# Order of the first stage in a retention and feed-forward kernel: token sums between the weight sums, clamps behind copies, a key transposed ahead of scores

## The chip, the cores and the metric

The kernel runs on one core of a Trainium2 chip. The metric is the device time of one execution in microseconds (us), the median of several runs. A profile of one further execution shows what every engine did: PE (matrix multiplies and transposes, with its weight loads as PEld), DVE (vector operations), ACT (scalar operations), POOL (GpSimd), and the DMA queues, of which SP's carries nearly all loads and stores.

## What is computed

The reference has two halves. The first is a retention layer over 8 batches, 8 heads, 576 positions and 64 values a head; its output becomes 4608 tokens of 512 values. The second is a feed-forward layer with a product of two projections.

```
scores = (q @ k.T) / sqrt(64)
ret    = (scores * Dmat) @ v        # Dmat[i, j] = gamma_h ** (i - j) for i >= j, else 0
x      = ret, heads side by side    # 4608 x 512
h      = ((x @ w1) * (x @ w2)) @ w3
out    = h @ w_out
```

The weights arrive as 64-bit floating point numbers, so the kernel has to convert them to 32 bits itself.

## The kernel before, in words

**Retention.** The 576 positions of a pair of batches are cut into five chunks, the first of 64 positions and four of 128. A *unit* g is one chunk of one pair (unit 0 to 4 are the first pair). `load` (L100) brings k, q and v of a unit by DMA from SP's queue, 512 KB each, into tiles of which there are two of each kind. The decay is split into factors: `scale` (L162) multiplies q and v by them, either as one POOL operation (L171) or as eight ACT operations (L169). `front` (L174) transposes k and q on PE (L184), eight transposes each, and copies the results to the tiles kT and qT with two ACT copies each (L187). `score` (L190) multiplies kT and qT (L199) and masks the scores on DVE (L202, four operations). `state` (L206) adds the unit's k and v to a running state on PE (L220) and copies it out on ACT (L224). `pv` (L227) makes the output of the unit from state, qT, masked scores and v (L248, L255), and ACT copies it to token tiles xT (L260).

**Weights.** `load_block` (L276) loads one block of raw weight words into one of five buffers, again by SP's queue. A generator, `conversion` (L358), turns a block into 32-bit numbers in five DVE steps: the exponent e (L319), the mantissa m in two steps (L323, L326), and the joining of both (L340, L349). Together with L326 it issues two clamps on ACT (L329, L330) that bound the exponent; L340 of the block needs them. From the fifth block on, the generator begins a block ahead: the three steps of block n + 1 come before the two last steps of block n, and behind the last one the load of a further block is issued (L353). `convert(n)` (L379) takes n steps; `convert_up_to(n)` goes on until n blocks are done.

**Up-projection.** The product with w1 and w2 is done by a Strassen-Winograd scheme of seven products for one third of a pair's tokens and one quarter `fp` of the columns. `strassen_weights(fp)` (L150) makes the weight sums S1, S2, S3, S4 on DVE (L152), with a `yield` after each two. `strassen_tokens` (L415) makes the four token sums T1, T2, T3, -T4 (L424), on POOL unless told otherwise. `up` (L433) issues the products in the order A11·B11, S2·T2, S3·T3, S1·T1, A22·(-T4), A12·B21, S4·B22, each of eight PE matmuls (L450); five of them are followed by a DVE sum (L455), and each such sum by `convert(conv)`, so that conversion is spread between the products, and by one entry of the list `aside`, which holds other work. Then DVE multiplies the two projections (L476), and a last `convert(conv)` follows (L477).

**Order.** Nothing is reordered by a scheduler: every engine runs its instructions in the order in which the program issues them and waits by semaphores for the others. The order of the first stage is written out by hand (L603 to L664). There PE's work alternates between units of the retention and calls of `up`; DVE has conversions, sums and masks; ACT has copies, clamps and scalings. PSUM tiles rotate through seven banks.

The part around the change, in its order: weight sums of the first quarter, `pv(1)`, the loads of unit 3, the token sums, the first `up`, the front of unit 2, the scores and state of unit 2, the front of unit 3, `pv(2)`, the loads of unit 4, state and scores of unit 3, the second `up`, `pv(3)`, and the front of unit 4.

Of the kernel before, what the change touches and what calls it, by code (L numbers as in the profile page):

```python
# [8 lines left out]
F32 = mybir.dt.float32  # L9
# [26 lines left out]
def kernel(  # L36
# [20 lines left out]
    P = 128  # L57
    NP = H // 2
# [3 lines left out]
    NC = (S + P - 1) // P  # L62
# [22 lines left out]
    pools = {}  # L85
# [46 lines left out]
    for c in (0, slice(1, NC)):  # L132
        n = short if c == 0 else P
# [8 lines left out]
    def A(fp, nm):  # L142

        h, m = divmod(fp, 2)
        if nm in ("S1", "S2", "S4"):
            return wS[h][:, ("S1", "S2", "S4").index(nm), m]
        r, f = {"A11": (0, 0), "A12": (1, 0), "A21": (0, 1), "S3": (0, 1), "A22": (1, 1)}[nm]
        return wA[h][:, :, 2 * r:2 * r + 2, m * QC + f * P:m * QC + f * P + P]

    def strassen_weights(fp):  # L150
        def tt(out, in0, in1, op):
            nc.vector.tensor_tensor(out=A(fp, out), in0=A(fp, in0), in1=A(fp, in1), op=op)  # L152

        tt("S1", "A21", "A22", ALU.add)
        tt("S2", "S1", "A11", ALU.subtract)
        yield
        tt("S3", "A11", "A21", ALU.subtract)
        tt("S4", "A12", "S2", ALU.subtract)
        live["S", fp] = True
        yield  # L160

    def scale(g, nm, scalar=False):  # L162
        c = g % NC
        sz = sizes[c]
        t, gam = live[nm, g], {"q": gq, "v": gk}[nm]
        t = t[:sz].rearrange("p (b h) d -> p b h d", b=2)
        if scalar:
            for h in range(H):
                nc.scalar.mul(t[:, :, h, :], t[:, :, h, :], gam[:sz, c, h:h + 1])  # L169
            return  # L170
        nc.gpsimd.tensor_tensor(  # L171
            out=t, in0=t, in1=gam[:sz, c].unsqueeze(1).unsqueeze(3).to_broadcast([sz, 2, H, D]), op=ALU.mult)

    def front(g, names="kq"):  # L174
        c = g % NC
        sz = sizes[c]
        for nm in names:
            src = live[nm, g]
            dst = pools["fr"].tile([P, 2, NP, P], F32, tag=nm + "T", name=nm + "T", bufs=1 if nm == "k" else 2)
            for b in range(2):  # L180
                tp = acc.tile([P, NP, P], F32, tag="acc", name="tp")
                for p in range(NP):
                    h = b * H + 2 * p
                    nc.tensor.transpose(tp[:, p, :sz],  # L184
                                        src[:sz, h:h + 2, :].rearrange("p a d -> p (a d)"),
                                        ident[:sz, :sz])
                nc.scalar.copy(dst[:, b, :, :sz], tp[:, :, :sz])  # L187
            live[nm + "T", g] = dst
# [38 lines left out]
    def pv(g):  # L227
        i, c = divmod(g, NC)
        sz = sizes[c]
        live["x", g] = True  # L230
        qT, vs, pm = live["qT", g], live["v", g], live["pm", g]

        parts = []
        for n in range(NB):
            lo, hi = max(starts[c], n * TB), min(starts[c] + sz, (n + 1) * TB)
            if lo < hi:
                m = i * NB + n
                if ("xT", m) not in live:
                    live["xT", m] = xps[m % 4 == 3].tile([P, NP, 2, TB], F32, tag="xT", name="xT")
                parts.append((live["xT", m], lo - n * TB, lo - starts[c], hi - lo))  # L240

        banks = [acc.tile([P, 2, 2, P], F32, tag="acc", name="xps") for r in range(2)]
        order = [(b, n) for b in range(2) for n in range(2)]
        if c > 0:
            for m, (b, n) in enumerate(order):
                for r, j in ((0, 0), (0, 1), (1, 0), (1, 1)):
                    p = 2 * r + n
                    nc.tensor.matmul(banks[r][heads[j ^ r], b, n, :sz], live["sb", g][heads[j], b, p, :],  # L248
                                     qT[heads[j], b, p, :sz], start=(m == 0), stop=False,
                                     skip_group_check=True)  # L250
        for m, (b, n) in enumerate(order):
            for r in range(2):
                for half in range(2):
                    p, j = 2 * r + n, half ^ r
                    nc.tensor.matmul(banks[r][heads[half], b, n, :sz], vs[:sz, b * H + 2 * p + j, :],  # L255
                                     pm[:sz, b, j, p, :sz], start=(c == 0 and m == 0), stop=True,
                                     skip_group_check=True)
        for x, to, fr, n in parts:
            for r in range(2):
                nc.scalar.copy(  # L260
                    x[:, 2 * r:2 * r + 2, :, to:to + n].rearrange("p n b s -> p b n s"),
                    banks[r][:, :, :, fr:fr + n])
# [116 lines left out]
    def convert(n):  # L379

        for _ in range(n):
            if go_on() is not None:
                return
# [31 lines left out]
    def strassen_tokens(i, n, engine=nc.gpsimd):  # L415

        m = every.index((i, n))
        x = live["xT", m]
        B = [[x[:, 2 * r:2 * r + 2, b, :] for b in range(2)] for r in range(2)]
        T = [(t_first if m == 1 and j == 2 else ffn).tile(  # L420
            [P, 2, TB], F32, tag="T", name="T", bufs=1 if m == 1 and j == 2 else 5) for j in range(3)]

        def minus(out, in0, in1):
            engine.tensor_tensor(out=out, in0=in0, in1=in1, op=ALU.subtract)  # L424

        live["B", i, n] = {"B11": B[0][0], "B21": B[1][0], "B22": B[1][1], "T3": B[0][1],
                           "T1": T[0], "T2": T[1], "-T4": T[2]}
        minus(T[0], B[0][1], B[0][0])
        minus(T[1], B[1][1], T[0])
        minus(B[0][1], B[1][1], B[0][1])  # L430
        minus(T[2], B[1][0], T[1])

    def up(i, n, fp, conv=0):  # L433
        m = every.index((i, n))
        while ("S", fp) not in live:
            assert go_on() is None
        if ("B", i, n) not in live:
            strassen_tokens(i, n)
        if fp == 0:
            live["ab", i, n] = (pools["ab3"] if m == 2 else ffn).tile([P, 2 * KF, TB], F32, tag="ab", name="ab")  # L440
        ab = live["ab", i, n]

        def product(ps, a, b):
            a, b = A(fp, a), live["B", i, n][b]
            new = ps is None
            if new:
                ps = acc.tile([P, 2, TB], F32, tag="acc", name="up")
            for w in range(2):
                for r in range(2):
                    nc.tensor.matmul(ps[:, w, :], a[:, w, r, :], b[:, r, :], start=(new and w == r == 0),  # L450
                                     stop=(w == r == 1), skip_group_check=True)
            return ps

        def plus(ps, to, sb):
            nc.vector.tensor_add(c[:, to], ps, c[:, sb])  # L455
            convert(conv)
            if aside:
                aside.pop(0)()


        c = ffn.tile([P, 4, 2, TB], F32, tag="c", name="c", bufs=1)
        p1 = product(None, "A11", "B11")
        nc.scalar.copy(c[:, 0], p1)
        plus(product(None, "S2", "T2"), 1, 0)
        plus(product(None, "S3", "T3"), 2, 1)
        p5 = product(None, "S1", "T1")
        plus(p5, 3, 2)
        plus(product(None, "A22", "-T4"), 2, 2)
        product(p1, "A12", "B21")
        nc.scalar.copy(c[:, 0], p1)  # L470
        product(p5, "S4", "B22")
        plus(p5, 1, 1)

        if fp == NQ - 1 and m + 1 < len(every) and has_x(*every[m + 1]) and ("B", *every[m + 1]) not in live:
            strassen_tokens(*every[m + 1])
        nc.vector.tensor_mul(ab[:, 4 * fp:4 * fp + 4, :], c[:, :, 0, :], c[:, :, 1, :])  # L476
        convert(conv)  # L477


    aside = []  # L480
# [148 lines left out]
    convert_up_to(3)  # L629
    load_block()  # L630
    convert_up_to(4)
    for _ in strassen_weights(0):
        pass
    pv(1)
    load(3, "kqv")
    load_block()
    strassen_tokens(0, 0, nc.vector)
    scale(2, "q", True)
    aside.append(lambda: scale(2, "v", True))
    up(0, 0, 0, conv=2)  # L640
    front(2)
    scale(3, "q", True)
    score(2)
    state(2)
    scale(3, "v", True)
    front(3)
    convert(2)
    pv(2)
    load(4, "kqv")
    state(3)  # L650
# [2 lines left out]
    score(3)  # L653
    aside.extend([lambda: None] * 3 + [lambda: scale(4, "q", True)])
    up(0, 0, 1, conv=2)
    pv(3)
    front(4)
    strassen_tokens(0, 1, nc.vector)
    score(4)
    aside.append(lambda: scale(4, "v", True))  # L660
# [89 lines left out]
    for g in range(NC, G):  # L750
        c = g % NC
        n = -(-len(todo) // (NC - c))
# [64 lines left out]
```

## Time and profile before

| | |
|---|---|
| runs | 894.08, 894.42, 895.47 us, median 894.42 |
| profiled execution | 892.5 us, span from first to last instruction 890.8 us |
| PE busy | 866.0 us, 97% of the span |
| DVE, ACT, POOL busy | 436.4, 214.7, 110.1 us |
| read from and written to memory | 49.32 and 9.44 MB |

An extract of the page shows the span in 40 slices of 22.3 us; each digit is the busy share of a slice in tenths.

```profile
PE   5789999999999999999999999999999999999998
...
DVE  5879998973543333533424433433533524434343
ACT  3666343553022222111121111111111111001000
POOL 3000020002002232102112102220300101000000
```

PE is not full in the first three slices only. A timeline lists instructions in order: start and length in us, engine, line, what is written and read, the count that was merged into one row, and in brackets the idle time of the engine before it with what ended it. A table of waits sums these idle times by the instruction that ended them.

### The profile page before, as it was taken

To read this page: it belongs to the slowest core of one execution; us is meant where nothing else is said; L and a number is where in the kernel's file an instruction comes from. 1 tells how busy PE (TensorE), PEld (TensorE's weight loads), DVE (VectorE), ACT (ScalarE), POOL (GpSimd) and SP (SyncE) were. 2 spreads that over 40 slices of the span, in tenths; PEclk is the share of its full clock that TensorE was granted. 3 is DMA by queue.
4 is the path that set the end of the run, shared out by engine and by line. 5 is a ranking of instruction groups with operands and counts; after the bars stand their busy time and mean duration, and the time that the engine had idled before them with its cause. 6 is when DMAs were issued, how large, how long until landed. Compare 5 with 4: busy or idle time off the path is not lost.

```text
span 890.8 us, 15262 instructions
## 1 busy us (share of the span) xinstructions
PE 866.0 (97%) x6517; PEld 792.3 (89%) x6517; DVE 436.4 (49%) x763; ACT 214.7 (24%) x434; POOL 110.1 (12%) x81
## 2 busy tenths in 40 slices
PE   5789999999999999999999999999999999999998
PEld 5779999655889999999999999999999999999997
DVE  5879998973543333533424433433533524434343
ACT  3666343553022222111121111111111111001000
POOL 3000020002002232102112102220300101000000
PEclk9999999999999999999999999999999999999999
DMA  9993322436035543134033043012100000000001
GB/s 201 218 211 85 107 93 97 136 125 106 1 80 119 120 76 72 25 72 95 1 71 60 3 94 86 9 44 53 25 24 24 1 25 1 24 24 1 24 1 47
DMA packets 125555, 59.73 MB, mean 67 GB/s; under 512 B 113704, under 2 KB 113704, under 8 KB 125488
## 3 DMA queue, kind: packets, MB, share of 16 engines
q1 hardware_dynamic: 123824, 58.47, 29.2%
q8 instruction: 51, 0.84, 0.4%
q10 hardware_dynamic: 1664, 0.30, 0.3%
q14 instruction: 16, 0.13, 0.0%
HBM read 49.32 MB, written 9.44 MB: 66 GB/s over the span
## 4 chain that ended last, share of the span: by engine, by line
PE 90%; DVE 4%; DMA 2%; ACT 2%; issue 1%; POOL 0%; SPq 0%; ACTq 0%; DVEq 0%
PE up L450 45%; PE po L555 24%; PE ps L405 6%; PE sc L199 4%; PE xps L255 4%; PE tp L184 3%; PE st L220 2%; PE xps L248 2%; DMA ld_q<-in_q_dram 1%; DMA dq<-decay_q_dram 1%; DVE c L455 1%; PE tp L395 1%; DVE e L340 1%; DVE wS L152 0%; ACT e L329 0%
## 5 line engine op out<-in xcount | busy, mean ns | idle before, releaser
L455 DVE TENSOR_TENSOR c<-up,c 128x384 f32<-128x384 f32 x240 | 133.5, 556 | 224.8 <-PE up L450 218.7
L450 PE MATMUL up<-xT,wA 128*128 128x192 f32 x1152 | 212.0, 327 | 0.7 <-ACT xT L260 0.7
L450 PEld LDWEIGHTS up<-xT,wA 128*128 128x128 f32 x1152 | 190.3, 190 | 3.0 <-ACT xT L260 0.9
L450 PE MATMUL up<-T,wS 128*128 128x192 f32 x768 | 140.6, 326 | 4.9 <-DVE T L424 3.3
L450 PEld LDWEIGHTS up<-T,wS 128*128 128x128 f32 x768 | 127.3, 190 | 5.4 <-issue 5.4
L555 PE MATMUL po<-w3o,ab 128*128 128x256 f32 x456 | 104.1, 380 | 0.3 <-ACT ot L577 0.3
L555 PEld LDWEIGHTS po<-w3o,ab 128*128 128x128 f32 x456 | 85.9, 190 | 12.2 <-ACT ot L577 0.7
L470 ACT COPY c<-up 128x384 f32<-128x384 f32 x48 | 22.9, 478 | 228.1 <-PE up L450 223.9
L559 DVE TENSOR_TENSOR ot<-po,ot 128x256 f32<-128x256 f32 x90 | 38.2, 424 | 74.9 <-PE po L555 74.2
L450 PE MATMUL up<-xT,wS 128*128 128x192 f32 x384 | 70.6, 327 | 0.6 <-DVE c L455 0.5
L202 DVE TENSOR_TENSOR pm<-sc,mask 128x512 f32<-128x512 f32 (+1 forms) x80 | 45.6, 629 | 51.2 <-PE sc L199 51.2
L450 PE MATMUL up<-T,wA 128*128 128x192 f32 x384 | 70.2, 326 | 0.0
L555 PE MATMUL po<-wB,forms 128*128 128x256 f32 x288 | 65.1, 379 | 0.0
L450 PEld LDWEIGHTS up<-xT,wS 128*128 128x128 f32 x384 | 63.6, 190 | 1.5 <-DVE c L455 1.5
L450 PEld LDWEIGHTS up<-T,wA 128*128 128x128 f32 x384 | 63.7, 190 | 0.0
L555 PEld LDWEIGHTS po<-wB,forms 128*128 128x128 f32 x288 | 54.7, 190 | 7.4
L405 PE MATMUL ps<-wo,w3T 128*128 128x512 f32 x128 | 56.4, 593 | 0.2 <-ACT w3T L397 0.2
L171 POOL TENSOR_TENSOR ld_q<-ld_q,gq 128x1024 f32<-128x1024 f32 (+1 forms) x17 | 33.1, 1948 | 189.0 <-DMA ld_q<-in_q_dram 181.4
L171 POOL TENSOR_TENSOR ld_v<-ld_v,gk 128x1024 f32<-128x1024 f32 (+1 forms) x17 | 32.8, 1928 | 174.7 <-DMA ld_v<-in_v_dram 145.4
L424 POOL TENSOR_TENSOR T<-xT,T 128x384 f32<-128x384 f32 x20 | 21.2, 1061 | 227.8 <-PE up L450 226.1
L405 PEld LDWEIGHTS ps<-wo,w3T 128*128 128x128 f32 x128 | 23.7, 190 | 27.3 <-issue 26.8
L476 DVE TENSOR_TENSOR ab<-c 128x768 f32<-128x768 f32 x48 | 46.0, 958 | 3.8
(72 smaller groups left out, 837.9 us busy)
## 6 DMA issues: line engine op xcount, KB each, us to landing
raw<-in_moe_w_dram SPq DMA_DIRECT2D x24, 512.0 KB, 3.8
ld_k<-in_k_dram SPq DMA_DIRECT2D x16, 512.0 KB, 6.0
ld_q<-in_q_dram SPq DMA_DIRECT2D x16, 512.0 KB, 7.4
ld_v<-in_v_dram SPq DMA_DIRECT2D x16, 512.0 KB, 5.0
out_dram<-ot SPq DMA_DIRECT2D x24, 256.0 KB, 2.1
raw<-in_moe_w_dram SPq DMA_DIRECT2D x16, 256.0 KB, 6.4
raw<-in_moe_w_out_dram SPq DMA_DIRECT2D x8, 512.0 KB, 3.4
out_dram<-ot SPq DMA_DIRECT2D x24, 128.0 KB, 2.4
```

The costliest lines, as they stand in the source:

```text
L171: nc.gpsimd.tensor_tensor(out=t, in0=t, in1=gam[:sz, c].unsqueeze(1).unsqueeze(3).to_broadcast([sz, 2, H, D]), op=ALU.mult)
L184: nc.tensor.transpose(tp[:, p, :sz], src[:sz, h:h + 2, :].rearrange("p a d -> p (a d)"), ident[:sz, :sz])
L199: nc.tensor.matmul(sc[j][:sz, p, :sz], kT[hs, b, p, :sz], qT[hs, b, p, :sz], start=True, stop=True)
L202: nc.vector.tensor_mul(pm[:sz, b, j, :, :sz], sc[j][:sz, :, :sz], mask[:sz, :sz].unsqueeze(1).to_broadcast([sz, NP, sz]))
L255: nc.tensor.matmul(banks[r][heads[half], b, n, :sz], vs[:sz, b * H + 2 * p + j, :], pm[:sz, b, j, p, :sz], start=(c == 0 and m == 0), stop ...
L405: nc.tensor.matmul(ps, live["w3T", ft][:, g, :], live["wo"][:, g, :], start=(g == 0), stop=(g == KF - 1))
L450: nc.tensor.matmul(ps[:, w, :], a[:, w, r, :], b[:, r, :], start=(new and w == r == 0), stop=(w == r == 1), skip_group_check=True)
L455: nc.vector.tensor_add(c[:, to], ps, c[:, sb])
L470: nc.scalar.copy(c[:, 0], p1)
L476: nc.vector.tensor_mul(ab[:, 4 * fp:4 * fp + 4, :], c[:, :, 0, :], c[:, :, 1, :])
L555: nc.tensor.matmul(ps[nm], a[A][:, f, :], live["W"][B][:, f, :], start=(f == 0 and not on), stop=(f == NP - 1), skip_group_check=True)
L559: nc.vector.tensor_add(ot[:, to[0], to[1]], ps[nm], ot[:, sb[0], sb[1]])
```

## The change

It edits the hand-written order of the first stage, and has four parts.

1. The weight sums of the first quarter are issued in two halves: S1 and S2, then `pv(1)`, the loads and the token sums as before, then S3 and S4.
2. The first `up` leaves out its last `convert(2)`. One of the steps (L326 with its two clamps) comes behind `front(2)`. The other steps of the stage are dealt out anew: two behind the transposes of k of unit 3, five in place of two behind the front of unit 3.
3. q of unit 3 is scaled on POOL instead of ACT, and k of unit 3 is transposed and copied before the scores of unit 2; its q follows after the state of unit 2. For the first pair kT has two tiles instead of one.
4. The front of unit 4 is issued before `pv(3)` instead of after it.

```diff
@@ front
-            dst = pools["fr"].tile([P, 2, NP, P], F32, tag=nm + "T", name=nm + "T", bufs=1 if nm == "k" else 2)
+            dst = pools["fr"].tile([P, 2, NP, P], F32, tag=nm + "T", name=nm + "T",
+                                   bufs=1 if nm == "k" and g >= NC else 2)
@@ up
-    def up(i, n, fp, conv=0):
+    def up(i, n, fp, conv=0, tail=True):
...
-        convert(conv)
+        if tail:
+            convert(conv)
@@ order of the first stage
     convert_up_to(4)
-    for _ in strassen_weights(0):
-        pass
+    first_sums = strassen_weights(0)
+    next(first_sums)
     pv(1)
     load(3, "kqv")
     load_block()
     strassen_tokens(0, 0, nc.vector)
+    for _ in first_sums:
+        pass
     scale(2, "q", True)
     aside.append(lambda: scale(2, "v", True))
-    up(0, 0, 0, conv=2)
+    up(0, 0, 0, conv=2, tail=False)
     front(2)
-    scale(3, "q", True)
+    convert(1)
+    scale(3, "q")
+    front(3, "k")
+    convert(2)
     score(2)
     state(2)
     scale(3, "v", True)
-    front(3)
-    convert(2)
+    front(3, "q")
+    convert(5)
     pv(2)
     load(4, "kqv")
     state(3)
...
     up(0, 0, 1, conv=2)
+    front(4)
     pv(3)
-    front(4)
     strassen_tokens(0, 1, nc.vector)
```

## The prediction

> **What bounds the kernel now.** I read the page first, then TensorE's waits, the windows by stage, and the timeline of all engines from 28 to 80 us.
>
> Windows by stage (columns: stretch, length, busy time and count of PE, PEld, DVE, ACT, POOL, granted clock, DMA share, GB/s):
>
> ```profile
> 47.00:48.50 1.50, 1.50 (x18) 1.50 (x18) 0.06 (x1) 1.50 (x7) 0.00 (x0) 0.50 1.05 302
> ...
> 62.00:130.00 68.00, 66.61 (x520) 64.55 (x521) 63.98 (x117) 30.79 (x62) 5.74 (x4) 1.00 0.32 96
> 130.00:890.80 760.80, 755.65 (x5450) 687.14 (x5448) 330.13 (x572) 147.06 (x293) 94.77 (x66) 1.00 0.23 52
> ```
>
> From 62 us on PE is busy almost without a hole, so the kernel ends when PE's row of work ends, and only PE's holes before that can be saved. The DMA share is 1 until 64 us: transfers of the first stage are a stream that runs full. At 47 us the clock is halved. PE's waits up to 130 us (total, times, longest):
>
> ```profile
> PE up L450 <- DVE T L424: 3.3, 1, 3.3
> PE sc L199 <- ACT qT L187: 2.8, 2, 2.2
> ...
> PE up L450 <- DVE wS L152: 1.6, 1, 1.6
> ```
>
> They lie at 31.3-34.6, 44.4-46.6, 75.0-75.7 and 60.6-62.15 us. The timeline (start, length, engine, line) shows how each arises:
>
> ```profile
> 32.67 0.68 DVE L152 TENSOR_TENSOR wS<-wA,wS 128x512 f32<-128x512 f32 x1
> ...
> 33.28 0.55 DVE L424 TENSOR_TENSOR T<-xT 128x384 f32<-128x384 f32 x1
> ...
> 34.64 1.54 PE L450 MATMUL up<-T,wS 128*128 128x192 f32 x8 [3.29 <-DVE T L424]
> ...
> 44.39 0.72 ACT L330 ACTIVATE e<-e,lim 128x512 int32<-128x512 int32 x1
> ...
> 45.02 1.05 ACT L187 COPY kT<-tp 128x512 f32<-128x512 f32 x2
> ...
> 46.62 3.51 PE L199 MATMUL sc<-qT,kT 64*128 64x128 f32 x32 [2.19 <-ACT qT L187]
> ...
> 59.13 0.69 DVE L340 SCALAR_TENSOR_TENSOR e<-raw,e 128x512 int32<-128x512 int32 x1 [2.71 <-ACT e L330]
> ...
> 62.15 1.54 PE L450 MATMUL up<-T,wS 128*128 128x192 f32 x8 [1.58 <-DVE wS L152]
> ```
>
> Product S2·T2 waits for T2, queued on DVE behind all four weight sums. The copies of kT wait behind two clamps. The second block's S2 waits for DVE, which waits 2.71 us for a clamp that stands on ACT behind 4.9 us of scalings and eight copies.
>
> **What the Trainium skill says.** "TensorE: Matmul & The Clock Gate", Part 1, says that an idle window of about 3.4 us halves the clock, and Part 4 that transposes do not count as busy. The trace agrees: transposes and hole fill 42.5-46.6, and the clock is at 0.50 from 47.0 to 50.0. "SBUF — State Buffer", Who interferes with whom: a VectorE operation with two SBUF inputs and a GpSimd operation that reads SBUF lock each other out whole; with one SBUF input it does not. The trace agrees:
>
> ```profile
> 17.45 1.96 POOL L171 TENSOR_TENSOR ld_q<-ld_q,gq 128x1024 f32<-128x1024 f32 x1 [3.44 <-DMA ld_q<-in_q_dram]
> 17.69 2.28 DVE L349 SCALAR_TENSOR_TENSOR wA<-m,e 128x512 f32<-128x512 f32 x1
> ...
> 23.04 1.90 POOL L171 TENSOR_TENSOR ld_v<-ld_v,gk 128x1024 f32<-128x1024 f32 x1 [3.63 <-DMA ld_v<-in_v_dram]
> ...
> 23.59 2.48 DVE L202 TENSOR_TENSOR pm<-sc,mask 128x512 f32<-128x512 f32 x4 [0.90 <-PE sc L199]
> ```
>
> L349 takes 2.28 us instead of 0.69; the masks (PSUM and one SBUF input) keep 0.62 each. "DMA: Bandwidth & Descriptors", Queues, rings and completion order: an engine consumes its ring in order. The landings agree: asked issue by issue, the third unit's k lands near 43.4 (32.6 + 10.8), its q near 45.7 (33.2 + 12.5), raw block 8 at 50.5, 9 at 52.7, 10 at 54.5, the fourth unit's k at 56.8, its q at 59.5: some 2.3 us for 512 KB. (Units, blocks counted from 0.)
>
> **The change, part by part**, in the profile's own time (span 890.8; timed 892.5; median of the runs 894.42; I take differences over to the median).
>
> *Token sums between the weight sums.* S1 and S2 stay at 30.74 and 31.46. Independent DVE operations of these shapes start 0.61 and 0.47 apart, T2 follows T1 by 0.65: T1 32.07, T2 32.72, done 33.28, and S2·T2 starts 0.15 later, 33.43 instead of 34.64: 1.21 gained. S3 then starts at 34.15 and ends 34.83; S3·T3 could start at 34.80, so it waits about 0.15. S4 (ends 35.4) delays the first sum of c to 35.4, still ahead of the 36.27 of before. **1.04 us**; the block's products end at 41.47 instead of 42.51.
>
> *Clamps behind copies, k of unit 3 ahead of the scores of unit 2.* The tail of the block (L326, two clamps, L340) leaves the front of ACT's queue, and the copies of kT and qT need only PE's transposes: about 42.1 to 44.1. PE has transposes k2, q2 (41.47-43.2), then k3. That must land first: 43.45, a new wait of 0.25. Eight transposes take 0.93; scores of unit 2 start at 44.5, when qT is there. The wait of 2.19 is gone, and with it the idle window: scores take 2.06 instead of 3.51, state 1.10 instead of 1.27, **1.62**. Net **2.19 + 1.62 − 0.25 = 3.56**. The 0.93 of transposes is only moved from 51.26. The second kT buffer lets its two copies go before the scores have read the first; a PSUM bank for them is free once L455 has read the last product (42.2). Its 4 KB per partition shift the tiles beside it; whatever reuses their space is first written at 115 us, when all of them are done: nothing.
>
> *Scaling q of unit 3 on POOL.* Eight ACT operations (2.45 us) become one on POOL, which is idle from 24.94 to 120.99. It starts with the landing, 45.7, and takes 1.95: transposes of q3 can start at 47.72, where PE is through with state 2 at 47.55. Cost **0.2**. DVE's L340 and L349 of block 5 end at 45.7, just before POOL locks; the masks that follow do not feel it.
>
> *The rest of the row up to S2·T2 of the second block.* From the transposes of q the trace needs 6.81 us to the next A11·B11 (52.19 to 59.00): 47.72 + 6.81 = 54.53, S2·T2 at 55.95. DVE: masks of unit 2 end 48.1; e, m, m (L319-326) of block 7, then L340 and L349 of block 6 end 50.9; block 8's three (landed 50.5) end 52.4. ACT: state copy 47.67, scaling v3 48.15 (v lands near 48.1, halfway between q3 and block 8) to 50.6, copies of qT 51.5, clamps of block 7 to 52.9. So L340 of block 7 at 52.95, L349, S1, and S2 done at 55.8. Both meet at 56.0 against 62.15: the wait of **1.58** is gone. Sum so far 1.04 + 3.56 − 0.2 + 1.58 = 5.98, against 6.15 read off directly.
>
> *Unit 4's front ahead of the products of unit 3.* 16 transposes on PE and four copies on ACT pass 64 matmuls and four copies of xT. The copies of qT are then done about 1 us before the scores want them: the wait of **0.65** at 75.67 goes. The copies of xT end 4.85 + 1.3 us after the block instead of 4.0, so DVE idles some 2 us before the token sums of (0,1); before it waited 1.28 and 0.33 there itself, and reaches its first sum of c 5.8 us earlier than before, inside the 6.6 of PE; later it has waits of 0.22, 0.78 and 0.21 to close this.
>
> *SP.* Block 11's load now stands ahead of unit 4's k, q, v and waits for L340 of block 6 (50.2); behind it the three loads start at 51.5, as before (51.37), and the stream has backlog until 54.5, so nothing starves; but q4 lands 2.2 later, 61.7. Its scaling on ACT (61.8-64.3) is done before its transposes at 64.95.
>
> **Sum:** 1.04 + 3.56 − 0.2 + 1.58 + 0.65 = **6.6 us**, 894.4 − 6.6 = **887.8**. DVE's own chain allows at most 5.8 + 1.2 = 7.0.
>
> **Rivals.**
> - *Locked DVE (0.15).* If L349 of block 5 comes after q3's landing (margin 0.6 us), POOL holds it until 47.65: masks end 50.8 instead of 48.1, S2 comes 2.1 us later. 6.6 − 2.1 = 4.5: 889.9. For it: 2.28 us at 17.69. Against: the margin.
> - *A wait comes back in part (0.25).* Transposes k2, q2, k3 still make 3.0 us without a counted matmul; if the window falls so, scores and state pay 1.5 again: 889.3. Or v3 lands at 49.5 rather than 48.1 (bounds: q3's 45.7, block 8's 50.5): ACT's chain moves S2 by 1.4: 889.2.
> - *Given back to DVE (0.05).* DVE is busy 63.98 of 68 us from 62 to 130, and PE waits for it (0.53) at 116.69. Had DVE not come forward too, PE would wait there: 894. Against: DVE's idle 2.43, 0.42 and 2.71 us before 60 are what the change removes.
> - *Slower (0.03): loads of unit 4 become the bound.* They stand on SP behind block 11, which waits for DVE; q4's transposes now stand ahead of 64 matmuls on PE. Each us that q4 lands after 62.4 is a us of PE; from 69.0 on the kernel is slower. At 70.5 it would be 895.9. It takes L340 of block 6 at about 58 rather than 50; only a late k3 (everything on PE stands behind its transposes) could do that.
>
> The main case has 0.52. Low end: DVE's 7.0 and 0.6 of the runs' own spread, 886.8. High end 890.4 takes in the locked DVE and the partial waits. The measurement tells 0.2% (1.8 us) from no change: faster 0.92, same 0.05, slower 0.03.
>
> **What would show it.** S2·T2 at 33.4; scores of unit 2 near 44.5 at full clock; POOL's scaling at 45.7 with masks of 0.62; transposes of q3 at 47.7; S2·T2 of the second block at 56.0 without a wait; no wait at the fourth scores. Wrong if L349 near 45 us takes 2 us, the clock is 0.50 after 45, or PE waits at the transposes of k3 or q4.

## The result, and the profile after

The changed kernel takes **887.84 us** (median of 6 runs, 886.46 to 888.24), the kernel before in the same session 894.47 (6 runs, 894.08 to 895.47): a ratio of 0.9921, 95% interval 0.9908 to 0.9934, or 6.6 us less. Line numbers rise by one from `front` on: L184 becomes L185, L199 L200, L349 L350, L450 L451.

The page of the changed kernel, profiled at 887.59 us (the span, PE's busy share, and PE's row of the 40 slices):

```profile
span 885.9 us, 15255 instructions
...
PE 866.6 (98%) x6517; PEld 792.8 (89%) x6517; DVE 433.7 (49%) x763; ACT 212.4 (24%) x426; POOL 111.1 (13%) x82
...
PE   5899999999999999999999999999999999999998
```

PE's busy time is 866.0 before and 866.6 after: nothing was computed faster, holes were closed, and nearly all of them in the second and third slice (7 and 8 before, 8 and 9 now). The windows by stage show where the rest stands:

```profile
34.00:37.00 3.00, 2.76 (x9) 2.79 (x10) 2.23 (x5) 2.26 (x8) 0.00 (x0) 0.58 1.01 225
47.00:48.00 1.00, 1.00 (x24) 1.00 (x22) 0.97 (x3) 0.97 (x3) 0.06 (x1) 1.00 1.42 246
62.00:130.00 68.00, 67.40 (x528) 65.59 (x527) 64.71 (x118) 32.65 (x64) 5.74 (x4) 1.00 0.40 111
130.00:885.90 755.90, 750.73 (x5420) 682.23 (x5418) 325.58 (x563) 145.19 (x290) 94.80 (x66) 1.00 0.23 52
```

From 130 us on PE idles 5.17 us (755.90 − 750.73), before 5.15: untouched. From 62 to 130 its idle time falls from 1.39 to 0.60. The clock at 47 us is full; but at 34 us, where it was full in the profile of before, it is 0.58. That is the first thing the prediction did not foresee. PE's row and what feeds it, from the timeline of all engines:

```profile
34.24 2.69 PE L451 MATMUL up<-T,wS 128*128 128x192 f32 x8 [2.09 <-DVE T L425]
...
45.54 1.06 PE L185 MATMUL tp<-ident,ld_k 128*128 128x128 f32 x8
...
46.53 2.06 PE L200 MATMUL sc<-qT,kT 64*128 64x128 f32 x32
...
47.34 0.69 DVE L350 SCALAR_TENSOR_TENSOR wA<-m,e 128x512 f32<-128x512 f32 x1
...
47.94 1.90 POOL L171 TENSOR_TENSOR ld_q<-ld_q,gq 128x1024 f32<-128x1024 f32 x1 [22.38 <-DMA ld_q<-in_q_dram]
47.95 2.48 DVE L203 TENSOR_TENSOR pm<-sc,mask 128x512 f32<-128x512 f32 x4
...
49.90 1.09 PE L185 MATMUL tp<-ident,ld_q 128*128 128x128 f32 x8 [0.23 <-POOL ld_q L171]
...
58.17 1.46 PE L451 MATMUL up<-T,wS 128*128 128x192 f32 x8
...
70.74 2.06 PE L200 MATMUL sc<-qT,kT 64*128 64x128 f32 x32
```

The hole ahead of S2·T2 is 2.09 instead of 3.29. The scores at 46.53, S2·T2 of the second block at 58.17 and the fourth scores at 70.74 carry no bracket: none of them waits. The transposes of q3 wait 0.23 for POOL.

### The profile page after: what moved, and what is told of

Same layout as the page of the kernel before. It is cut to its first block, busy times and chain, and to the rows that moved or that the text cites. A ratio compares the mean times of both kernels' runs of the same rounds, so it can differ in the third digit from the quotient of the medians.

```text
span 885.9 us, 15255 instructions
## 1 busy us (share of the span) xinstructions
PE 866.6 (98%) x6517; PEld 792.8 (89%) x6517; DVE 433.7 (49%) x763; ACT 212.4 (24%) x426; POOL 111.1 (13%) x82
## 4 chain that ended last, share of the span: by engine, by line
PE 89%; DVE 3%; issue 1%; DMA 1%; ACT 1%; ACTq 0%; SPq 0%; DVEq 0%
PE up L451 45%; PE po L557 24%; PE ps L406 6%; PE xps L256 4%; PE sc L200 3%; PE tp L185 3%; PE xps L249 2%; PE st L221 1%; DVE c L456 1%; PE tp L396 1%; DVE e L341 0%; DMA raw<-in_moe_w_dram 0%; ACT e L330 0%; DVE w L350 0%; DVE ab L477 0%
## 5 line engine op out<-in xcount | busy, mean ns | idle before, releaser
L451 PE MATMUL up<-xT,wA 128*128 128x192 f32 x1152 | 212.6, 328 | 0.9 <-ACT xT L261 0.9
L451 PEld LDWEIGHTS up<-xT,wA 128*128 128x128 f32 x1152 | 191.0, 191 | 3.2 <-ACT xT L261 1.1
L451 PE MATMUL up<-T,wS 128*128 128x192 f32 x768 | 141.7, 328 | 2.1 <-DVE T L425 2.1
L451 PEld LDWEIGHTS up<-T,wS 128*128 128x128 f32 x768 | 128.3, 191 | 2.4 <-issue 2.4
L451 PE MATMUL up<-xT,wS 128*128 128x192 f32 x384 | 70.6, 327 | 0.6 <-DVE c L456 0.5
L451 PE MATMUL up<-T,wA 128*128 128x192 f32 x384 | 70.3, 326 | 0.0
L451 PEld LDWEIGHTS up<-xT,wS 128*128 128x128 f32 x384 | 63.6, 190 | 1.5 <-DVE c L456 1.5
L451 PEld LDWEIGHTS up<-T,wA 128*128 128x128 f32 x384 | 63.7, 190 | 0.0
L477 DVE TENSOR_TENSOR ab<-c 128x768 f32<-128x768 f32 x48 | 46.4, 967 | 3.8
```

## The experiments

My theory after the result: each step works as forecast, and the total is their sum. The rival: the total is right although its parts are not, because gains cover each other (the load stream and the lock between DVE and POOL set the row, whatever is freed beside them) and because the clock's windows changed. All medians stand beside runs of the kernel before on the same chip (894.54 to 894.73 by group); "changed" is 886.82 to 887.84.

**1 and 2. Both kernels once more.** No edit.

> The kernel before, unchanged, for a second profile. Its first profiled execution took 892.5 us, 2 us less than the median of its runs (894.47), while the changed kernel's took 887.59, its median 887.84. Theory A (the executions differ in the stream of loads: in the first profile q of unit 3 landed near 45.7 us, in the changed kernel's at 47.8): a profile near 894.4 us shows that landing at 47 us or later. Theory B (they differ in when the clock is halved): the landing is again near 45.7 and two windows of half clock show instead of one.

> The changed kernel, unchanged, beside the following ones: 6.6 us below the kernel before (886.5 to 889). In its first profile the clock was halved from 34.2 us for one window of 3.4 us, which cost 1.8 us on PE; the hole ahead of it (2.1 us) is shorter than the 3.3 us of before. If this belongs to the kernel, the half clock is there again and the scores of unit 2 start near 46.5; if it is a matter of phase, this execution may show none, with the scores near 44.7 and a time of about 886.5.

The changed kernel took 886.82 (ratio 0.992, 0.9908 to 0.9932). The kernel before, profiled at 892.17, is not the execution near 894.4 that either theory was about. Still, theory A's late landing cost nothing: q of unit 3 landed near 47.5 (asked for at 33.86, 13.6 us before) instead of 45.7, and the time is no longer (892.17 against 892.5). The execution had the three waits again (2.19, 1.58, 0.65), but its half clock elsewhere. Its windows:

```profile
34.00:37.00 3.00, 2.56 (x8) 2.59 (x9) 1.23 (x3) 1.17 (x4) 0.00 (x0) 0.50 1.03 240
47.00:50.40 3.40, 2.52 (x50) 2.40 (x52) 1.60 (x4) 3.40 (x11) 0.00 (x0) 1.00 1.02 241
```

In the first profile of the changed kernel the clock stays at 0.50 from about 34.5 to 37.9. A window of 3.4 us at half clock lowers the mean clock of an 890 us span by 3.4 × 0.5 / 890 = 0.002. So the mean clock, which every run has, should count them:

| mean clock | windows | before, 58 runs: runs, median us | changed, 11 runs: runs, median us |
|---|---|---|---|
| 1.000 | 0 | 0 | 6, 886.7 |
| 0.998 | 1 | 13, 892.26 | 5, 888.24 |
| 0.996 | 2 | 34, 894.59 | 0 |
| 0.994 | 3 | 10, 895.30 | 0 |
| 0.992 | 4 | 1, 896.58 | 0 |

The profile of run 3 below, with a mean clock of 0.996, does show two:

```profile
33.50:35.00 1.50, 1.50 (x6) 1.50 (x7) 1.50 (x4) 1.50 (x7) 0.00 (x0) 0.50 0.99 217
...
47.00:50.00 3.00, 3.00 (x28) 3.00 (x30) 0.95 (x2) 2.73 (x9) 0.00 (x0) 0.51 1.00 261
```

So the typical run of before has two windows; the profile that the prediction was read from had one, like 13 of these 58 runs. A window goes with 0.7 to 2.3 us by these rows; that it costs as much is not shown. The change takes away about one and a half of them on average; the sum had one.

The execution of the changed kernel that was profiled in run 2 had none at all. Its PE in the timeline, after the hole:

```profile
33.20 1.54 PE L451 MATMUL up<-T,wS 128*128 128x192 f32 x8 [2.09 <-DVE T L425]
...
42.18 1.04 PE L185 MATMUL tp<-ident,ld_q 128*128 128x128 f32 x8
44.58 1.06 PE L185 MATMUL tp<-ident,ld_k 128*128 128x128 f32 x8 [1.36 <-DMA ld_k<-in_k_dram]
45.57 2.06 PE L200 MATMUL sc<-qT,kT 64*128 64x128 f32 x32
...
48.97 1.09 PE L185 MATMUL tp<-ident,ld_q 128*128 128x128 f32 x8 [0.26 <-POOL ld_q L171]
...
57.24 1.51 PE L451 MATMUL up<-T,wS 128*128 128x192 f32 x8
```

S2·T2 runs at full clock, so PE reaches the transposes of k3 early and waits 1.36 us for the load; in the first profile the half clock had filled that time. The two profiles with one and no window, set against each other, close the account (us): hole ahead of S2·T2 3.19 − 2.09 = 1.10; from S2·T2 to the transposes of k2 9.33 − 8.11 = 1.22 (at full clock the order of before needs 42.51 − 34.64 = 7.87 there, so the half clock is 1.46, and the new order of sums gives back 0.24); scores 2.19; k3 −1.36; q3 −0.26; S2 1.58; fourth scores 0.65. Sum 5.12; the spans differ by 890.5 − 885.3 = 5.2. The typical run of before has a window more, 894.59 − 892.26 = 2.3, and about half the runs of the changed kernel have one, 0.5 × (888.24 − 886.7) = 0.8: 5.2 + 2.3 − 0.8 = 6.7.

**3. The token sums alone, put into the kernel before.**

```diff
-    for _ in strassen_weights(0):
-        pass
+    first_sums = strassen_weights(0)
+    next(first_sums)
...
     strassen_tokens(0, 0, nc.vector)
+    for _ in first_sums:
+        pass
```

> The kernel before with the token sums between the weight sums and nothing else. My theory: the first block's products 1.0 us earlier, the chain of clamps, copies and scalings behind them moves along, 1.0 us below before. Rival (the stream of loads and ACT set the second block's S2): the 1.0 us is lost again by S2.T2 of the second block, 0.0 to 0.2 below before.

892.83 (19 runs, 890.45 to 893.63), ratio 0.9984 (0.9976 to 0.9993): 1.7 below, the interval reaching from 0.6 to 2.1. The forecast 1.04 lies in it, the rival's 0 to 0.2 does not. Windows do not explain it: at a mean clock of 0.996 the medians are 892.93 here and 894.59 before. PE's waits of this kernel (what was waited for: total, times, longest):

```profile
PE sc L199 <- ACT qT L187: 2.8, 2, 2.2
PE up L450 <- DVE T L424: 2.1, 1, 2.1
PE up L450 <- DVE wS L152: 1.6, 1, 1.6
```

The hole shrinks from 3.3 to 2.1, and the later waits stay whole.

**4. The changed kernel without the new token sums.** S3 and S4 go back directly behind S1 and S2.

```diff
-    next(first_sums)
+    for _ in first_sums:
+        pass
...
-    for _ in first_sums:
-        pass
```

> The changed kernel with S3 and S4 back directly behind S1 and S2. My theory (PE's own row sets the end of the first stage): S2.T2 of the first block 1.2 us later, scores of unit 2 1.0 us later, transposes of q3 without a wait, time 5.6 us below before, 0.9 to 1.0 above the changed kernel. Rival (the landing of q3 and its scaling on POOL set the row from the transposes of q3 on): PE only uses up its wait there, time as the changed kernel, 6.6 below before.

889.56 (886.35 to 890.59), ratio 0.9943 (0.9927 to 0.9959): 1.7 to 2.7 above the changed kernel, more than the hole accounts for. Part of the surplus goes with the clock: two of these six runs have a mean of 0.996, none of the changed kernel's, and at 0.998 the medians are 889.46 and 888.24. The timeline of all engines shows another part:

```profile
47.73 2.34 POOL L171 TENSOR_TENSOR ld_q<-ld_q,gq 128x1024 f32<-128x1024 f32 x1 [22.99 <-PE tp L185]
...
48.34 2.28 DVE L350 SCALAR_TENSOR_TENSOR wA<-m,e 128x512 f32<-128x512 f32 x1
...
50.54 2.47 DVE L203 TENSOR_TENSOR pm<-sc,mask 128x512 f32<-128x512 f32 x4
...
60.18 1.54 PE L451 MATMUL up<-T,wS 128*128 128x192 f32 x8 [1.17 <-DVE wS L152]
```

DVE reaches L350 0.61 us after POOL has begun; it takes 2.28 instead of 0.69, and S2·T2 of the second block waits 1.17. That is the rival of the locked DVE, from the prediction, in a variant.

**5. The same without the scaling of q of unit 3** (this part of the computation is left out), to see whether POOL is the cause.

```diff
-    scale(3, "q")
```

> The kernel without the split of the weight sums (889.56), leaving out the scaling of unit 3's q, so that POOL does nothing between 25 and 110 us and can hold no DVE operation there; in that kernel PE had no wait for q3. The run that moved L350 behind the masks settled nothing: q3 landed earlier in it, and POOL held L477 for 2.67 us instead. Theory (the lock is the cause of the 1.0 us beyond PE's own row): no DVE operation of over 1.3 us but the masks, the wait for S2 (1.17) falls to 0.3 or less, and 0.8 to 1.2 below that kernel, 888.4 to 888.8. Rival (the loss belongs to the half clock or to another wait): within 0.4 of it, 889.2 to 890.

888.27 (887.93 to 889.23), ratio 0.9933 (0.9919 to 0.9947): by medians 1.3 below run 4, by the ratios 0.9, with intervals that overlap; at equal mean clock 1.4 (888.07 against 889.46 at 0.998, 888.95 against 890.38 at 0.996). DVE's timeline:

```profile
47.94 0.69 DVE L350 SCALAR_TENSOR_TENSOR wA<-m,e 128x512 f32<-128x512 f32 x1
48.55 2.48 DVE L203 TENSOR_TENSOR pm<-sc,mask 128x512 f32<-128x512 f32 x4
```

L350 is back at 0.69, and S2·T2 of the second block starts at 58.61 without a wait, 1.57 earlier; 0.40 of this was there before, at A11·B11 (57.05 against 57.45). With POOL's operation gone both are gone: the lock is shown. Its price in this row is the wait of 1.17; the times agree with it, within their spread.

**6. Run 4 with L350 behind the masks**, another way round the lock: one step fewer before `score(2)` and one more behind it.

```diff
-    convert(2)
+    convert(1)
     score(2)
...
-    convert(5)
+    convert(6)
```

> The kernel without the split of the weight sums (it took 889.56, 1.7 to 2.7 above the changed one, where PE's row alone gives 1.0), with one more edit: L350 of block 5 comes behind the masks of unit 2 instead of ahead of them. Theory (the missing 1.0 us is the lock: POOL's scaling of q3 held L350 at 48.34 for 2.28 us, which made S2 of the second block 1.2 us late): no DVE operation of over 2 us between 44 and 60, no wait for S2, and 0.8 to 1.2 below that kernel, about 888.5. Rival (the loss has another cause, such as the clock): within 0.4 of it.

889.29 (887.95 to 889.86), ratio 0.9942 (0.993 to 0.9954). Inconclusive: q3 landed earlier in the profile, POOL ran at 45.49, and another operation was held (timeline):

```profile
45.49 2.04 POOL L171 TENSOR_TENSOR ld_q<-ld_q,gq 128x1024 f32<-128x1024 f32 x1 [20.69 <-DVE e L320]
45.67 2.67 DVE L477 TENSOR_TENSOR ab<-c 128x768 f32<-128x768 f32 x1
```

L477 takes 2.67 instead of 0.95. Between 44 and 48 us DVE has two-input operations almost without a gap; which of them POOL holds depends on when q3 lands.

**7. The transposes of k3 back behind the scores and the state of unit 2**, with one kT buffer.

```diff
-                                   bufs=1 if nm == "k" and g >= NC else 2)
+                                   bufs=1 if nm == "k" else 2)
...
-    front(3, "k")
     convert(2)
...
-    front(3, "q")
+    front(3)
```

> The changed kernel with k of unit 3 transposed together with its q, behind the state of unit 2, and one kT tile. My theory: eight transposes (0.93 us) are only moved; scores of unit 2 start 0.9 earlier at about 43.7 in the time of the first profile, as soon as qT is there, with a hole of some 0.3 ahead; behind the state PE has k3's transposes while it waits for q3: within 0.3 us of the changed kernel, 6.3 to 6.6 below before. Rival (the transposes ahead of the scores hide the wait for the copies, and the single kT tile makes k3's copies wait for the scores): 0.7 to 1.5 above the changed kernel.

887.62 (886.71 to 888.07), ratio 0.9921 (0.9909 to 0.9933): no difference. The scores start at 45.20 behind a wait of 0.34 for qT, not 2.19: with the clamps moved, k3's place makes no difference that these runs tell. (In this execution POOL also held L341 of DVE for 2.40, and S2·T2 of the second block waited 0.31.)

**8. The clamps back ahead of the copies**, k3 staying ahead of the scores.

```diff
-    up(0, 0, 0, conv=2, tail=False)
+    up(0, 0, 0, conv=2)
     front(2)
-    convert(1)
...
     front(3, "k")
-    convert(2)
+    convert(1)
```

> The changed kernel with the tail of the first block (L327 with two clamps, L341) back ahead of the copies of kT and qT. My theory: the copies start 1.3 to 1.5 us later, behind the second clamp; k3's transposes hide 0.9 of that; scores of unit 2 some 0.8 later, and their wait before q3's transposes is used up: 0.6 to 0.9 above the changed kernel. Rival (the row from q3 on is set by q3's landing): less than 0.3 above it.

887.74 (886.64 to 888.2), ratio 0.9924 (0.9911 to 0.9937): no difference either; my 0.6 to 0.9 failed. PE's timeline:

```profile
44.60 1.06 PE L185 MATMUL tp<-ident,ld_k 128*128 128x128 f32 x8 [1.22 <-ACT kT L188]
45.60 2.06 PE L200 MATMUL sc<-qT,kT 64*128 64x128 f32 x32
47.58 1.15 PE L221 MATMUL st<-ld_v,ld_k 128*64 128x64 f32 x32
48.99 1.09 PE L185 MATMUL tp<-ident,ld_q 128*128 128x128 f32 x8 [0.25 <-POOL ld_q L171]
```

Within 0.03 us it is the row of run 2. The bracket names a copy, but the start is that of run 2, where the same transposes waited for the load. k3 landed near 44.5 in both (10.8 us after it was asked for at 33.68 and 33.63): PE stands there for k3, and the late copies fit into that time. So the two halves of this part do one job: either of them alone keeps the scores from waiting 2.19. A kernel with neither, beside the other parts, was not tried.

**9. k2 transposed ahead of A11·B11**, to put PE work into the hole, and k3 late as in run 7.

```diff
+    front(2, "k")
     strassen_tokens(0, 0, nc.vector)
...
-    front(2)
+    front(2, "q")
```

> The changed kernel with k of unit 2 transposed ahead of A11.B11 of the first block, in the hole before it, and k of unit 3 behind the state of unit 2 (as in the run that put it there). Theory (from the transposes of q3 on the row is set by the loads, and what PE gains ahead of it is worth only the half clock that it prevents): the hole ahead of S2.T2 falls from 2.1 to about 1.2 us, every run shows a clock of 1.0, median 886.3 to 886.9. Rival 1 (PE's own row sets the end): 0.9 below the best runs of the changed kernel (886.5), 885.6. Rival 2 (the window of half clock belongs to the low activity of the whole first 34 us, not to this hole): half of the runs stay at 0.998 and the median at 887.6.

888.07 (887.86 to 888.27), ratio 0.9932 (0.992 to 0.9943): no gain, and my 886.3 to 886.9 failed. The transposes fill the time ahead of A11·B11; the hole ahead of S2·T2 stays at 2.02, because T2 on DVE still ends it. POOL began the scaling of q3 at 46.17, so that L350 at 46.73 was held for 2.27. The forecast of full clock in every run failed too: two of the five have a mean of 0.998. They took 887.86 and 888.07, the three with 1.000 took 887.93 to 888.27: here a window goes with no time at all.

**10. k and q of unit 3 loaded ahead of a raw block**, to end the wait for k3.

```diff
     convert_up_to(3)
+    load(3, "kq")
     load_block()
     convert_up_to(4)
...
-    load(3, "kqv")
+    load(3, "v")
```

> The changed kernel with the loads of unit 3's k and q issued ahead of raw block 7's instead of behind it (v stays behind). Theory (the full stream of loads sets where the row resumes: PE waited 1.36 us for k3's landing at 44.6 and 0.26 for POOL's scaling of q3, which starts as q3 lands at 47.0): both land 2.3 us earlier, PE does not wait for k3, and the scaling ends before PE is through with unit 2's state. But POOL then starts near 44.7 and holds DVE's L341 or L350 of block 5 for up to 1.9 us, and block 8 still lands when it did: S2.T2 of the second block gains 0.5 us at most, 0 to 0.5 below the changed kernel. Rival (the two waits are all there is): 1.2 to 1.6 below the changed kernel. Second rival (the lock costs more than the landing gains): 0.5 to 1.5 above it.

887.74 (886.98 to 888.73), ratio 0.9927 (0.9915 to 0.9939): no gain. PE no longer waits for k3, but q3 lands earlier too (timelines of PE, of POOL and DVE):

```profile
44.80 1.04 PE L185 MATMUL tp<-ident,ld_k 128*128 128x128 f32 x8
...
44.86 2.25 POOL L171 TENSOR_TENSOR ld_q<-ld_q,gq 128x1024 f32<-128x1024 f32 x1 [19.88 <-DMA ld_q<-in_q_dram]
45.27 2.39 DVE L327 SCALAR_TENSOR_TENSOR m<-raw,m 128x512 f32<-128x512 uint32 x1
```

L327 is locked, and S2·T2 of the second block waits 1.3: what the load gives, the lock takes.

**11. q of unit 3 scaled on ACT again.**

```diff
-    scale(3, "q")
+    scale(3, "q", True)
```

> The changed kernel with q of unit 3 scaled by eight ACT operations in the same place. My theory: 2.45 us come back into ACT's queue ahead of the copies of kT3, the state's copy, v3's scaling, the copies of qT3 and the clamps of block 7, which wait for q3's landing as well: L341 of block 7 and with it S2.T2 of the second block 1.8 us later, 1.5 to 2.0 above the changed kernel. Rival (ACT has room, POOL's lock on DVE costs as much): within 0.4 us of the changed kernel.

888.23 (887.21 to 888.74), ratio 0.9927 (0.9915 to 0.9939): 0.4 to 1.4 above the changed kernel, between my 1.5 to 2.0 and the rival's 0.4; at equal mean clock 0.6 (1.000) and 0.3 (0.998). The timeline of all engines:

```profile
46.16 2.43 ACT L169 ACTIVATE ld_q<-ld_q,gq 128x128 f32<-128x128 f32 x8
...
54.73 0.69 DVE L341 SCALAR_TENSOR_TENSOR e<-raw,e 128x512 int32<-128x512 int32 x1 [1.38 <-ACT e L331]
...
57.74 1.54 PE L451 MATMUL up<-T,wS 128*128 128x192 f32 x8 [0.99 <-DVE wS L152]
```

The old chain is back in part: ACT's scalings delay a clamp, DVE waits 1.38 for it, PE 0.99 for S2. In exchange PE waits neither for POOL nor, in this execution, for k3: S2·T2 starts 0.5 after that of run 2.

**12. The front of unit 4 behind `pv(3)` again.**

```diff
-    front(4)
     pv(3)
+    front(4)
```

> The changed kernel with the front of unit 4 back behind pv of unit 3. My theory: the scores of unit 4 wait again for the copies of qT (0.65 us before), and the token sums of (0,1) come 2 us earlier without use to PE: 0.65 above the changed kernel, 5.9 to 6.0 below before. Rival (DVE, busy 94% from 62 to 130 us, sets that stage, and the later copies of xT cost it 2 us): this kernel is as fast as the changed one or up to 0.5 faster.

887.79 (886.46 to 889.82), ratio 0.9928 (0.9916 to 0.9941). By medians between 0 and 1.0 above the changed kernel; with equal mean clock 887.57 against 886.7 (1.000) and 889.49 against 888.24 (0.998), so 0.9 and 1.3. In PE's timeline the wait is back:

```profile
72.67 1.60 PE L200 MATMUL sc<-qT,kT 64*128 64x128 f32 x23 [0.65 <-ACT qT L188]
```

That these times are the price of this wait is not shown: in the same execution POOL held a DVE operation, and S2·T2 of the second block waited 1.29.

```profile
46.45 2.39 DVE L341 SCALAR_TENSOR_TENSOR e<-raw,e 128x512 int32<-128x512 int32 x1
```

No version tried is faster than the changed kernel. The theory of steps that add up fits run 3. For the clamps and the loads (runs 8 and 10) the rival fits better: undoing the one or adding the other moves the time by less than the runs of one kernel differ. The hole ahead of S2·T2 goes with the clock as well. Where it is 2.0 to 2.1 in the profile (the changed kernel and runs 7 to 12), 19 of 43 runs have a mean clock of 1.000; where it is 3.29 (runs 4 to 6), 1 of 17.

## Why the prediction was right, and where its terms were wrong

The total held: 6.6 us forecast, 6.6 measured. One of the signs that the prediction named for being wrong did come in run 2, PE's wait at the transposes of k3. By its steps:

- **Token sums.** Forecast 1.04: 1.21 at the hole less what S3·T3 waits, with S2·T2 at 33.4. Run 2 has it at 33.20 and 1.10 at the hole; 0.24 goes again behind it, so 0.86 is left. Alone (run 3) the edit gives 1.7, with the forecast inside the interval; why it is more than the hole is open. Right in kind and nearly in size.
- **Scores of unit 2.** That the wait of 2.19 would go was right. Two terms of the 3.56 were mis-sized. "That must land first: 43.45, a new wait of 0.25" measured 1.36 in run 2 and no wait in the first profile, where the half clock had made PE late. The landing was read from one profile, and that one had the earliest stream of the four of these two kernels. k3 was asked for at 32.64 in the profile of before (33.21 in run 1, 34.49 in the first profile of the changed kernel); in run 2:

```profile
33.63 0.55 SPq L106 DMA_DIRECT2D ld_k<-in_k_dram  x1
```

  From there to the landing it is 10.8 us, as long as in the prediction; only the start is later. In run 1 it was 11.8. The other term is the half clock, forecast as one window of 1.62 that disappears. In its place stand one and a half fewer on average, with which 1.46 + 2.3 − 0.8 = 3.0 goes by the account above, and the one that is left in the first profile follows the hole at 34 us. Nor does the wait of 2.19 always bring a window: in run 1 transposes and hole fill 43.77 to 47.88 just the same, and the clock behind them is 1.00. The errors, 1.1 too little of wait for k3, 1.4 too little of half clock and 0.2 too much of token sums, cancel: that the total fits so closely is partly luck.
- **q of unit 3 on POOL.** Forecast a wait of 0.2 with masks of 0.62 beside POOL. Measured 0.23 and 0.26, and four masks in 2.48. Right in size, though POOL starts at 47.01 and 47.94 instead of 45.7: k3 and q3 came late together. Taken alone it is rather a gain than a cost, since it takes the scalings off ACT (run 11), but the times of run 11 hardly tell it from nothing.
- **S2 of the second block.** Forecast: DVE and PE meet at 56.0, the wait of 1.58 gone. It is gone in both profiles, at 57.24 and 58.17; S2 was done 0.2 to 0.3 us earlier (in run 2 at 57.06). A meeting as close as forecast, and therefore one that nearly every later edit broke: runs 4, 6, 7, 9, 10, 11 and 12 show a wait for S2 again, 0.3 to 1.3.
- **Front of unit 4.** Forecast 0.65; the wait is gone, and back at 0.65 when undone (run 12). Right as a wait; what it is worth in time, run 12 does not tell.
- **SP and q4.** Forecast a landing at 61.7 and "each us that q4 lands after 62.4 is a us of PE". The loads of unit 4 went out at 52.61 (run 2) and 53.80 (first profile) instead of 51.5, and in both profiles the scaling of q4 waited for the landing until 64.0. In run 2:

```profile
64.01 2.45 ACT L169 ACTIVATE ld_q<-ld_q,gq 128x128 f32<-128x128 f32 x8 [1.03 <-DMA ld_q<-in_q_dram]
```

  PE lost only 0.28 (eight transposes in 1.32 instead of 1.04). The rule was too strict: eight transposes of k4 come first, and those of q4 start at 65.96, before the last of the eight scalings ends at 66.46. The slower rival, which lived on this, did not come about.

**The rivals.** The wait that comes back in part did, in other places than named: half clock at 34 us in the first profile, 1.36 for k3 in run 2. The locked DVE did not occur in the two profiles of the changed kernel: L350 begins 0.60 ahead of POOL in one (47.34 and 47.94), 2.16 ahead in the other. It occurs in six variants (runs 4, 6, 7, 9, 10 and 12), where an operation takes 2.27 to 2.67 us, so it does hang on half a microsecond, as forecast. Its price, 2.1 us at S2, was too high: S2·T2 waits 0.3 to 1.3 there. The Trainium skill, "SBUF — State Buffer", Who interferes with whom, says that the order of issue decides who blocks; the runs agree: in run 4 L341 began 0.12 ahead of POOL and took 0.69, and POOL 2.34 instead of 1.90; L350, behind POOL, took 2.28. Given back to DVE: PE's idle time from 62 to 130 us fell instead.

**Still open:** why the load stream starts up to 1.9 us later in one of these four executions than in another (0.6 and 0.9 between two of the same kernel), what a half-clock window costs by itself, and what the clamps and k3's early transposes are worth together, since each alone was enough.

## What to carry to other kernels

Before a saving is read off one profile, see which run it was: here the mean clock of every run told how many half-clock windows it had, and the landing time of k3 in a full load stream moved by 1 to 2 us between executions (43.4 to 45.4), so it deserves such a margin. Gains around one meeting point don't add up: here the loads, the copies on ACT, DVE's conversions and POOL's lock meet ahead of S2·T2 of the second block, and freeing one ran into the next (runs 9 and 10). Work moved to POOL can hold DVE's two-input operations that start behind it (0.69 became 2.28 here, with a wait of up to 1.3 on PE); look at what DVE issues in the 2 us around its start, for the earliest and the latest landing.

## What was not expected of the hardware

- **Half clock can follow a hole of 2.09 us.** The Trainium skill, "TensorE: Matmul & The Clock Gate", Part 1, speaks of an idle window of about 3.4 us, and of windows that run free of the program. Here holes of 0.88 and 2.09 with eight matmuls (1.57 us) between them were followed by half clock in one execution, holes of 0.56 and 2.09 in another were not. The first hole does not decide: 0.82 and 2.09 in run 8 were not followed by it, 0.52 and 2.09 in run 3 were. That the same order gives either fits the free-running window; that PE need not be idle for all of 3.4 us (0.88 + 2.09 = 2.97, with work between) is what the trace adds.
- **Half clock and a wait can take each other's place.** From the start of A11·B11 the transposes of k3 begin 14.96 us later in the first profile (30.58 to 45.54) and 15.04 in run 2 (29.54 to 44.58). Between S2·T2 and the transposes of k2 the half clock cost the first one 9.55 − 8.11 = 1.44; the other waited 1.36 for the load. In the first profile k3 landed near 45.4 (34.49 + 10.9), so at full clock PE would have waited for it too: by this estimate the window cost next to nothing there, and the 0.6 between the two spans (885.9 and 885.3) comes with the start of A11·B11, 1.04 later in the first.
